# A recurrent attention block and an expert layer on one core: heads 0 to 3 and 4 to 7 in the two partition halves, read weights turned by way of DRAM, and new queue orders

## The chip, the cores and the metric

The kernel runs on one core of a Trainium2 chip. The metric is the device time of one launch in microseconds. Three runs of the kernel before took 720.58, 729.39 and 728.37 us, a median of 728.37.

A core has five engines that run side by side, each with a queue of its own: TensorE (PE, matmuls, with weight loads shown as PEld), VectorE (DVE), ScalarE (ACT), GpSimd (POOL) and SyncE (SP). SyncE computes nothing here; its queue issues most of the transfers, GpSimd's some, ScalarE's two at the start. All transfers run on the same 16 DMA engines.

## What is computed

```python
def _attn_ref(x, state):            # x (8, 8, 512, 64), state (8, 8, 32, 64)
    scale = 1.0 / np.sqrt(D)
    scores = scale * np.matmul(x, state.transpose(0, 1, 3, 2))
    a = softmax(scores)
    xread = np.matmul(a, state)
    scores2 = scale * np.matmul(state, x.transpose(0, 1, 3, 2))
    a2 = softmax(scores2)
    sread = np.matmul(a2, x)
    return np.concatenate([xread, sread], axis=2)

x = attn_out.transpose(0, 2, 1, 3).reshape(B * S, H * D)    # 4352 x 512
h = x @ w_in                        # 512 x 2048
g = h * erf(softplus(h))
out = g @ w_out                     # 2048 x 512
```

`softmax` stands for the usual steps (subtract the maximum of the row, exponentiate, divide by the sum plus 1e-9). The two weight matrices arrive as 64-bit floats.

## The kernel before

Eight batches are worked one after the other. A batch has 8 heads of 512 tokens and 32 states. Two heads fill the 128 partitions of the head dimension (2 x 64): before, heads 2i and 2i+1 are the pair i, head 2i in partitions 0 to 63 and head 2i+1 in partitions 64 to 127. Four heads of 32 states fill 128 partitions on the side of the states.

**Attention of a batch** (`attend`, L667 to L759). The tokens come in a form that VectorE can turn with its 32 by 32 transpose: `load_xq` (L88 to L93) makes 16 transfers for a batch, one for each head and each half of the head dimension, each of 64 KB in pieces of 32 elements. Each then is turned in place (L676), TensorE forms the scores (`score`, L684) and ScalarE copies them to `sc` (for odd batches) or to a part of `m` (for even ones). One softmax runs over the states of a token and one over the tokens of a state; the weights of the second (L724) are turned in 32 by 32 blocks (L746), and the blocks must then be exchanged between partition groups. `send` (L749 to L756) does it with 16 transfers of 32 KB from `xT` to `sc` or `m`. `read` (L773 to L792, matmul in L782) multiplies the turned weights with the tokens in a second layout, `x`, loaded by `load_x_static` (L765 to L768), 8 transfers a batch, one for each head.

**Expert layer.** `mixed` (L811, matmul in L820) multiplies the states with `w_in` first, so that the product with the softmax weights (`first_product`, L919) gives h directly. `serf` (L956, L959) forms h times erf of softplus of h. The second product runs in `second_product` (L1003) or, for the later batches, in `twice_product` (L1239). Both products use Strassen-like sums of blocks (`sums_y` L857, `sums_a` L970, and others), so VectorE has many adds.

**Weights.** A 64-bit weight is turned to 32 bits by two ScalarE and three VectorE instructions (`convert`, L542 to L550). The first half is fetched at the start on SyncE's queue (`fetch_pair`; `fetch_in` L525, `fetch_out` L533, and L559), the second half later on GpSimd's, in stages of one piece.

**The order of the work.** Nothing is issued where it stands in the code. `op` (L139) records each step with its engine, a cost, what it reads and what it writes. At the end `emit` (L291) walks five hand-given orders, one for each engine (`ORDER`, L163), in which the numbers are places in that engine's list of steps, and gives each step a time of beginning from the costs: a transfer may have a landing time (`land`) or a shared one (`pipe`: the transfers that have it pass one after the other). The instructions are then recorded in the order of these times, and `in_order` (L78) ties each engine to its order. So the costs decide no more than how the five orders interleave in the program; each engine's own order is that of `ORDER`. `either` (L156) gives some copies to VectorE (`BY_VECTOR`), the rest to ScalarE. Spare products (`spare_products`) keep TensorE busy at the start, before there is real work.

SyncE's queue is in order: a transfer that waits for its data, or for its destination to come free, holds all that are behind it. In the stretch that matters here, before, it holds the 16 transfers of `load_xq` for batch 2, 8 of `load_x_static` for batch 1, the 16 of `send` for batch 1, `kept_a` and `kept_y` (L864 and L865, which keep a batch's products for the second half of the kernel), the 16 of `load_xq` for batch 3, and so on in turn.

Of the kernel before, what the change touches and what calls it, by code (L numbers as in the profile page):

```python
# [17 lines left out]
def kernel(  # L18
# [17 lines left out]
    nc = tc.nc  # L36
# [51 lines left out]
    def load_xq(b, hs=range(H)):  # L88
        t = xq_t[b]
        for h in hs:  # L90
            i, e = h // 2, h % 2
            for k in range(2):
                nc.sync.dma_start(  # L93
                    out=t[D * e + Ns * k:D * e + Ns * k + Ns, i],
                    in_=x[b, h, :, Ns * k:Ns * k + Ns].rearrange("(m t) d -> t m d", t=Ns))
# [13 lines left out]
    where = {h: (g, q) for g, hs in enumerate(((0, 2, 1, 3), (5, 7, 4, 6)))  # L109
             for q, h in enumerate(hs)}  # L110
# [28 lines left out]
    def op(engine, cost, at, go, reads=(), writes=(), table=None, land=0.0, pipe=0.0):  # L139
# [14 lines left out]
        x2 st s01 m010 m011 m020 m021 u0 u1 m120""".split())  # L154

    def either(name, cost, out, in_, at, reads, writes):  # L156
# [3 lines left out]
        else:  # L160
# [4 lines left out]
            8 0 5 1-3 6 15 9 4 7 10 12 16 13 17 11 14 18 20-21 19 23 25 24 22 61 60 53 52 44-45 37  # L165
            26 46 28 27 29 36 47 62 31-32 30 54 68 48-49 51 50 34 33 41 35 38 69 40 70 55 39 43 72
            63 42 73 65 74 84 71 75 77 76 66 79-80 78 67 81 85 64 59 57 56 86 93 82-83 97 87 98 89
            88 58 94-96 90 99 101-102 121 100 122 124 103 123 125 109 105-106 128 126-127 107 131 91
            108 132 130 110 129 133 92 113-114 134 104 115 111 116 135 112 136 117-120 138 140-141
            168 142-143 171 144 169 145 170 146 148 172 147 149-150 137 175 173 151 156 178 139 174  # L170
            179 152-154 180 176 155 157 181 177 160-163 182 158-159 183 185 187 164-167 188-189 215
            190 216 191 218 195 217 184 219 199-200 220 201-202 192 221-222 193 196 225 194 186 197
            203 226 223-224 227 198 228-229 204-205 230 207-208 206 209 232 263 210 262 234-235 265
            236 231 266 211-212 264 237 233 267-269 213 270 272 271 214 273 242 246-248 238-239 275
            249 243 274 277 244-245 276 240-241 250-256 281 257 282-283 279 258 284 259 309 278 260
            289 312 261 311 313 290 310 285 314 316 291 315 293-294 318 295 286 280 319 296 287 320
            317 288 292 322 321 297 301 323 302-303 324 355 298-300 356 304 357 327 305-308 362 358
            329 328 334 359 325 335-336 330 360 337 326 331 338 361 365 339 364 332 366 340 363 367
            348 368 350 397-398 333 349 399 341 351 342-343 352 344-345 354 346 353 376 401 377-378
            400 379 347 380 402 369 381-382 371 370 373 403 372 404 374 390 405 375 406 383 392 409  # L180
            407 385 408 391 384 410 393-394 387 427 425 386 388 395 426 389 428 396 431-432 429
            433-434 413 430 415 435-436 423 437 416 421 438-439 414 440 455 419 424 457 422 458 456
            411 420 412 417 459 418 462 461 460 445 443 465 463 441 466 444 464 467-468 449 469 442
            470 453 447 454 450 448 499 446 451 502 501 452 478 500 503 471 506 480 473 504 472 479
            482 481 505 509 508 475 474 510 483 507 484 476 511 477 512-513 485 492 487 514 489
            493-494 543 495 486 488 546 490 545 496 491 544 498 547 497 522 515 550 549 517 548
            523-524 516 519 553 552 518 526 554 520 525 555 551 527-528 521 556 536 529 538 557-558
            531 530 537 540 539 533 587 532 534 542 589 541 566 588 568 567 590 570 535 571 591 559
            594 561 592-593 560 569 562 596-597 563 572 598 595 564 599-600 580 565 601 581-582 573
            602 583 631 575 574 584 576-577 634 633 578 585 579 586 603 635 610 632 605 636 611 604  # L190
            606 613 638 612 607 637 614 641 639-640 642 616 615 609 643 608 617 624 644-645 626 646
            625 619 675 618 628 627 621 620 629 676 678 630 677 679 622 654 623 655-656 680 682 658
            657 647 681 648 685 683-684 686 659 650 649 687 651 660 688-689 652-653 668 690 670 669
            661 720 719 672 671 721 662-664 673-674 665 722 666 726 723 698 667 700 699 701 724 702
            725 691 729 693 728 730 704 727 695 703 692 732 696 694 731 734 712 697 733 714 713 763
            715 705 716 765-766 707 706 718 717 764 767 708 770 709 768 710 742 711 743-744 769 735
            746 772 745 737 773 771 739 736 774 740 738 747 775 748 776 756 741 758 749 757 759 751
            750 752-753 760 754-755 762 777 761 784 778-779 786 781 780 785 782-783 788 791 787 793
            792 794-795 790 789 797-798 796 805 799-801 807 802 806 808-809 803-804 810-811""",
        ACT: """  # L200
            0-3 5 14-15 4 12-13 7 6 8 16 10 17 32-33 18-19 55 9 11 56 20-21 35 34 36 38 22-23 37 39
            24-25 41 40 26-27 43 42 44-45 28-29 47 49-50 46 48 64 53 61 58 57 51-52 54 59 66-67 65
            68-69 31 60 70 73 71 95 94 105 104 72 77 74 102-103 76 106 75 107 79 86-87 78 98 63 96
            80 100 97 99 83 82 101 81 84-85 90 135 88 91 134 136-137 145 110 139 62 138 109 89 92
            149 30 93 108 151 112 142 113 150 152 111 153 158 154-155 160 143 140 147 161 141 159
            163 115 156 162 114 164 144 166 146 157 148 165 172 171 116 167-168 173-174 176 175 186
            117-118 169 119 170 182 188 187 120 189 121 180 190 195 177 179 197 178 198 122 183 123
            191 194 181 192 201 184 124 199 125 202 196 200 203 193 204 185 208-209 205 210 212 211
            126 128 206 213 207 127 223 219 217 225-226 224 131 129 216 227 215 214 130 229 232 132
            234-235 133 233 238 236 230 220 239 218 221 237 240 228 231 246-247 245 248 241 249 242  # L210
            250 260 222 243 262 244 263 255 261 264 269 256 271 254 252 272 253 251 266 277 258 265
            268 270 273 267 274 276 284 282 285 275 278-280 257 281 259 283 287 286 293 297 299 290
            298 300 288 291 301 306 289 302 308 304 292 309 312 307 295 311 310 303 314 313 305 319
            315 321 320 322 294 316-317 344 296 318 324 345-346 329 347 325 348 330-331 323 353 327
            332 350 326 349 355 354 351 333 356 352 357 359 339 358 360 340 361-363 328 364 334 365
            335 342 341 386 337-338 336 343 371 373 372 374 366 375 367 369 388 368 381 370 389 382
            376 387 390 393 392 391 377 394-395 384 396 379 397 378 380 385 383 399 401 398 402-403
            400 406 405 413 412 415 414 417 404 407-411 418 422 419-421 426 424 428 425 429 423 427
            432 431 430 433-436 441 440 437 439 442 416 463 438 465 448 464 443 466 449 467 472 450
            444 451 473-474 446 475 445 471 469 476 479 447 486 453 480 452 468 454 458 477 470 478  # L220
            488 485 487 481 509 482 456 459 511 455 483 461 460 510 484 512 462 494 457 489 513 518
            490 515 495 492 520 491 514 521 516 497 493 496 517 524 519 498 522-523 525 504-505 526
            499 527 533-534 528 531 500 507 529 532 506 502 555 530 508 540 501 541 556-557 543 503
            558 535-536 559 564-565 544 542 566 538 563 567 561 537 560 570 569 568 550 562 571-573
            577 539 574 545 580 579 578 551 575 546 552 576 553 601 548 547 602 549 554 603 581 604
            586 582 607 588 605 610 608 584 587 589 583 612-613 585 611 615 591 614 590 606 596-597
            623 616 618 625-626 609 617 592 619 598 624 599 620 647 621 593 649 622 594 600 648 650
            632-633 651 634 595 627 635 656 658 657 659 653 628 654 660 636 629 652 630 662 669 631
            670 642 663 661 672 671 664 655 643 665 693 645 637 666 644 667 694 638 646 668 640 639
            695 641 696 678 680 679 697 681 702 673 704 674 699 705 708 682 676-677 703 701 675 706  # L230
# [1464 lines left out]
```

## Time and profile before

| | |
|---|---|
| runs | 720.58, 729.39, 728.37 us; median 728.37 |
| profiled execution | 719.11 us, its span 717.3 us, mean granted TensorE clock 0.99 |
| TensorE busy | 698.8 us, 97% of the span |
| VectorE busy | 593.4 us, 83% |
| ScalarE busy | 471.9 us, 66% |
| GpSimd busy | 85.7 us, 12% |
| transfers | 159615 packets, 89.22 MB, of them 124096 packets under 512 bytes |
| chain that ended last, by engine | PE 82%, DVE 4%, SyncE's queue 4%, DMA 1%, ACT 1% |
| `load_xq`, SyncE | 112 transfers of 64 KB, 3.1 us from issue to landing (median) |
| `load_x_static`, SyncE | 56 of 128 KB, 3.6 us |
| `send`, SyncE | 64 of 32 KB to `sc`, 1.9 us, and 48 to `m`, 2.0 us |
| `kept_a`, SyncE | 8 of 512 KB, 3.9 us |

The busy times of engines overlap. A busy TensorE row counts matmuls that are in the pipeline, so two instructions that overlap are not counted twice. Idle time of an engine that is not the limit costs nothing. The granted clock is the share of full speed at which TensorE was let run.

### The profile page before, as it was taken

To read this page: it belongs to the slowest core of one execution; us is meant where nothing else is said; L and a number is where in the kernel's file an instruction comes from. 1 tells how busy PE (TensorE), PEld (TensorE's weight loads), DVE (VectorE), ACT (ScalarE), POOL (GpSimd) and SP (SyncE) were. 2 spreads that over 40 slices of the span, in tenths; PEclk is the share of its full clock that TensorE was granted. 3 is DMA by queue.
4 is the path that set the end of the run, shared out by engine and by line. 5 is a ranking of instruction groups with operands and counts; after the bars stand their busy time and mean duration, and the time that the engine had idled before them with its cause. 6 is when DMAs were issued, how large, how long until landed. Compare 5 with 4: busy or idle time off the path is not lost.

```text
span 717.3 us, 13372 instructions
## 1 busy us (share of the span) xinstructions
PE 698.8 (97%) x5163; PEld 581.6 (81%) x5163; DVE 593.4 (83%) x989; ACT 471.9 (66%) x850; POOL 85.7 (12%) x93
## 2 busy tenths in 40 slices
PE   8899979999999999999999999999999999999997
PEld 7434647788787868789999779898989898989996
DVE  4999969999999899697975479686969587789797
ACT  4996976978767575657444765667585577676732
POOL 0001100111001000000100100013222104312321
PEclk9899998999999999999999999999999999999999
DMA  8858596989576934240486402124545503735485
GB/s 271 204 142 189 125 229 162 235 206 237 92 192 219 255 82 132 48 131 1 119 198 225 92 0 81 52 30 91 80 81 60 101 11 85 104 42 67 58 141 104
DMA packets 159615, 89.22 MB, mean 124 GB/s; under 512 B 124096, under 2 KB 147520, under 8 KB 159040
## 3 DMA queue, kind: packets, MB, share of 16 engines
q1 hardware_dynamic: 140208, 58.22, 31.5%
q0 software_dynamic: 18800, 29.63, 22.2%
q8 instruction: 41, 0.67, 0.4%
q10 hardware_dynamic: 544, 0.52, 0.2%
q14 instruction: 22, 0.18, 0.1%
HBM read 47.19 MB, written 37.49 MB: 118 GB/s over the span
## 4 chain that ended last, share of the span: by engine, by line
PE 82%; DVE 4%; SPq 4%; DMA 1%; ACT 1%; issue 1%; DVEq 0%; ACTq 0%
PE o L1239 30%; PE h L919 17%; PE o L1003 15%; PE at L919 7%; PE o L1422 3%; PE h L1373 3%; SPq L93 2%; PE h L820 2%; PE at L820 2%; SPq L754 1%; PE h L684 1%; PE at L1373 1%; PE at L782 1%; DVE ring L970 1%; PE o L622 1%
## 5 line engine op out<-in xcount | busy, mean ns | idle before, releaser
L931 ACT COPY ring<-h 128x512 f32<-128x512 f32 x120 | 69.5, 584 | 80.2 <-PE h L919 69.4
L919 PE MATMUL h<-aT,m 128*128 128x256 f32 x360 | 92.1, 382 | 0.1
L959 DVE TENSOR_TENSOR ring<-ring 128x1024 f32<-128x1024 f32 (+1 forms) x64 | 72.9, 1150 | 18.1 <-ACT ring L956 18.0
L941 ACT ACTIVATE ring<-ring 128x512 f32<-128x512 f32 x120 | 72.3, 631 | 10.9 <-PE o L1003 2.6
L1003 PE MATMUL o<-w_out,ring 128*128 128x256 f32 x320 | 77.6, 383 | 1.3 <-DVE ring L959 1.3
L919 PEld LDWEIGHTS h<-aT,m 128*128 128x128 f32 x360 | 65.4, 190 | 12.7 <-issue 1.8
L1003 PEld LDWEIGHTS o<-w_out,ring 128*128 128x128 f32 x320 | 60.1, 191 | 16.5 <-issue 3.0
L970 DVE TENSOR_TENSOR ring<-ring 128x1024 f32<-128x1024 f32 x60 | 72.9, 1216 | 0.3
L1239 PE MATMUL o<-w_out,w_in 128*128 128x128 f32 x512 | 69.2, 276 | 0.0
L1239 PEld LDWEIGHTS o<-w_out,w_in 128*128 128x128 f32 x512 | 64.5, 192 | 1.9 <-issue 0.3
L1239 PE MATMUL o<-w_out,ring 128*128 128x128 f32 x480 | 65.1, 276 | 0.0
L1239 PEld LDWEIGHTS o<-w_out,ring 128*128 128x128 f32 x480 | 60.5, 192 | 4.3 <-issue 0.8
L956 ACT ACTIVATE ring<-ring 128x1024 f32<-128x1024 f32 (+1 forms) x64 | 63.3, 1008 | 0.2
L1003 PE MATMUL o<-raw,ring 128*128 128x256 f32 x240 | 59.2, 386 | 0.0
L1003 PEld LDWEIGHTS o<-raw,ring 128*128 128x128 f32 x240 | 45.5, 192 | 11.2 <-issue 3.4
L1239 PE MATMUL o<-raw,ring 128*128 128x128 f32 x360 | 48.5, 275 | 0.0
L1239 PEld LDWEIGHTS o<-raw,ring 128*128 128x128 f32 x360 | 45.3, 192 | 1.7 <-DVE oo L1254 0.8
L1159 POOL DMA_DIRECT2D out_dram<-oo x16 | 24.4, 1585 | 151.1 <-ACT ring L956 115.0
L1239 PE MATMUL o<-raw,xT 128*128 128x128 f32 x320 | 41.7, 276 | 0.0
L1239 PEld LDWEIGHTS o<-raw,xT 128*128 128x128 f32 x320 | 38.8, 192 | 2.1 <-ACT o L1270 1.7
L622 PE MATMUL o<-w_out,ring 128*128 128x512 f32 x64 | 31.0, 607 | 0.1
L919 PE MATMUL at<-sy,sx 128*128 128x256 f32 x120 | 31.0, 381 | 0.0
(267 smaller groups left out, 1401.1 us busy)
## 6 DMA issues: line engine op xcount, KB each, us to landing
xq<-in_x_dram SPq DMA_DIRECT2D x112, 64.0 KB, 3.1
x<-in_x_dram SPq DMA_DIRECT2D x56, 128.0 KB, 3.6
out_dram<-oo SPq DMA_DIRECT2D x10, 512.0 KB, 3.7
raw<-in_moe_w_in_dram SPq DMA_DIRECT2D x8, 512.0 KB, 6.9
raw<-in_moe_w_out_dram SPq DMA_DIRECT2D x4, 1024.0 KB, 6.5
raw<-in_moe_w_out_dram POOLq DMA_DIRECT2D x8, 512.0 KB, 6.0
raw<-in_moe_w_in_dram POOLq DMA_DIRECT2D x8, 512.0 KB, 6.7
kept_a<-aT SPq DMA_DIRECT2D x8, 512.0 KB, 3.9
```

What stands on the lines that cost most here:

```text
L622: nc.tensor.matmul(out=bank("o%d" % r), lhsT=gT[g][:, i, P * r:P * r + P], rhs=w_out[:, GF * g + i, :], start=(made_of[r] == 1), stop=(mad ...
L820: nc.tensor.matmul(out=bank(names[k])[Ns * p:Ns * p + Ns, :], lhsT=st[r, b, q], rhs=of_group[2 * u + j][r, :, i, :], start=True, stop=True)
L919: nc.tensor.matmul(out=out_[:, i], lhsT=x_[:, q:q + P], rhs=y_, start=(start and i == 0), stop=(i == 1), skip_group_check=not start)
L931: op(ACT, 0.5, t, lambda: nc.scalar.copy(out_(), view(bank(name))), [name], w)
L941: op(ACT, 0.53, t, lambda: nc.scalar.activation(out=part(splane, k), in_=part(hplane, k), func=ACTF.Softplus), area(hplane, ks=[k], os=[o] ...
L956: op(ACT, 0.085 + 0.875 * share, at + n, lambda s_=s_: nc.scalar.activation(out=s_, in_=s_, func=ACTF.Erf), [], area(splane, ks=[k], os=os ...
L959: op(DVE, 0.065 + 1.075 * share, at + n + 1, lambda s_=s_, h_=h_: tt(s_, s_, h_, op=ALU.mult), area(hplane, ks=[k], os=os), area(splane, k ...
L970: op(DVE, 1.14, at + k, lambda k=k, x_=x_, y_=y_, how=how: tt(get("h", k), get(*x_), get(*y_), op=how), area(v[x_[0]], ks=[x_[1]]) + area( ...
L1003: nc.tensor.matmul(out=view(name)[:, h], lhsT=lhs[:, i, :], rhs=weight_of[n]()[:, u, i, :], start=(start and h == 0 and i == 0), stop=(h = ...
L1159: op(GP, 1.2, t, lambda: nc.gpsimd.dma_start(out=quad(r, c), in_=one(v), accum_op=ALU.add), every(*v), [("out", b, r, c)], land=6.0)
L1239: nc.tensor.matmul(out=out_[:, Q2 * k:Q2 * k + Q2], lhsT=lhs[:, k, i], rhs=rhs[:, i], start=first, stop=(k == len(ns) - 1 and i == 1), ski ...
L1373: nc.tensor.matmul(out=bank(bk)[:, P * i:P * i + P], lhsT=x_[:, i, k], rhs=y_[:, k], start=(start and i == 0 and k == 0), stop=(i == GF - ...
```

## The change

It has four parts.

1. **Heads.** Heads 0 to 3 now lie in partitions 0 to 63 and heads 4 to 7 in partitions 64 to 127, so that pair i is heads i and 4+i. One transfer can then load four heads: `load_xq` makes 4 transfers for a batch instead of 16, the states of batches 1 to 7 come in 2 instead of 8, and the rows of `w_in`, which have to follow the heads, in two halves of 64 partitions for each piece instead of one transfer of 128 partitions. The tokens in the layout of `read` come two heads at a time, 4 transfers instead of 8.
2. **Read weights.** The exponentials of the second softmax are written in another order, so that after the 32 by 32 turn one transfer puts the whole `xT` half (128 x 1024) into a DRAM tile, `kept_t`, and four transfers bring it back, each to 32 partitions. These replace the 16 transfers from `xT` to `sc` or `m`.
3. **Costs of transfers in the plan.** Nearly all transfers get a share of a common DMA time (`pipe`) instead of a landing time of their own, and SyncE's queue is held to 4 us ahead of it (`AHEAD`).
4. **Orders.** All five orders in `ORDER` and the list `BY_VECTOR` are new. The same matmuls, and but for the transfers nearly the same instructions, stand in other places.

The core of the diff (the five orders, which make up most of it, and changed costs left out):

```diff
-    def load_xq(b, hs=range(H)):
+    def load_xq(b, first=0, n=NI):
         t = xq_t[b]
-        for h in hs:
-            i, e = h // 2, h % 2
+        for e in range(2):
             for k in range(2):
+                q, h = D * e + Ns * k, NI * e + first
                 nc.sync.dma_start(
-                    out=t[D * e + Ns * k:D * e + Ns * k + Ns, i],
-                    in_=x[b, h, :, Ns * k:Ns * k + Ns].rearrange("(m t) d -> t m d", t=Ns))
+                    out=t[q:q + Ns, first:first + n].rearrange("t i m d -> t (i m) d"),
+                    in_=x[b, h:h + n, :, Ns * k:Ns * k + Ns].rearrange(
+                        "i (m t) d -> t (i m) d", t=Ns))
...
     BY_VECTOR = set("""
-        x2 st s01 m010 m011 m020 m021 u0 u1 m120""".split())
+        x0 x1 x2 s10 ta1 m021 u1""".split())
...
-    FIXED = 2.6
+    FIXED, AHEAD = 2.2, 4.0
...
                     if pipe:
-                        piped = max(piped, end[n]) + pipe
-                        end[n] = piped + FIXED
+                        piped = max(piped, begin[n]) + pipe
+                        end[n] = max(piped, free[e]) + (land or FIXED)
+                        if e == SP:
+                            free[e] = max(free[e], piped - AHEAD)
...
+    def rows_in(on, to, f, n):
+        for e in range(2):
+            on.dma_start(out=to[D * e:D * e + D],
+                         in_=moe_w_in[NI * D * e:NI * D * (e + 1), P * f:P * (f + n)].rearrange(
+                             "(k d) f -> d k f", d=D).bitcast(U32))
...
-            for h in range(4 * k, 4 * k + 4):
-                i, e = h // 2, h % 2
-                nc.sync.dma_start(out=st[Ns * i:Ns * i + Ns, 1:B, D * e:D * e + D],
-                                  in_=state[1:B, h].rearrange("b n d -> n b d"))
+            nc.sync.dma_start(out=st[:, 1:B, D * k:D * k + D],
+                              in_=state[1:B, NI * k:NI * k + NI].rearrange(
+                                  "b i n d -> (i n) b d"))
...
             op(ACT, 0.7, at + 6, lambda e=e: nc.scalar.activation(
-                out=both()[:, 2 + e], in_=sc()[:, e], func=ACTF.Exp,
+                out=both()[:, 2:4].rearrange("p k t -> p (k t)").rearrange(
+                    "p (m e c n) -> p e c m n", m=NI, e=2, c=NC)[:, e],
+                in_=sc()[:, e].rearrange("p (c m n) -> p c m n", c=NC, m=NI), func=ACTF.Exp,
                 bias=m2()[:, e:e + 1], scale=scale, accum_out=z2()[:, e:e + 1]),
...
         def send():
-            blocks = both()[:, 0:2].rearrange("p e (c m n) -> p m (e c) n", m=NI, n=Ns)
-            rows = sc().rearrange("p e (c i n) -> p i (e c) n", c=NC, n=Ns)
+            nc.sync.dma_start(out=kept_t[b % 2], in_=both()[:, 0:2].rearrange("p k t -> p (k t)"))
+
+        def receive():
+            blocks = kept_t[b % 2].rearrange("(i t) (m x) -> m t i x", t=Ns, m=NI)
             for m in range(NI):
-                for i in range(NI):
-                    nc.sync.dma_start(out=rows[Ns * m:Ns * m + Ns, i],
-                                      in_=blocks[Ns * i:Ns * i + Ns, m])
-
-        op(SP, 11.0, at + 10, send, ["xT0", "xT1"], [sc_of(b, 0), sc_of(b, 1)], land=4.0)
+                nc.sync.dma_start(out=square()[Ns * m:Ns * m + Ns], in_=blocks[m])
+
+        op(SP, 0.5, at + 10, send, ["xT0", "xT1"], ["kt%d" % (b % 2)], pipe=1.4)
+        op(SP, 2.1, at + 14, receive, ["kt%d" % (b % 2)], [sc_of(b, 0), sc_of(b, 1)], pipe=1.7)
...
-        for h in range(H):
-            nc.sync.dma_start(out=t[:, :, h, :], in_=x[b, h].rearrange("(c p) d -> p c d", p=P))
+        for h in range(0, H, 2):
+            nc.sync.dma_start(out=t[:, h:h + 2].rearrange("p h c d -> p (h c) d"),
+                              in_=x[b, h:h + 2].rearrange("h (c p) d -> p (h c) d", p=P))
```

In the changed kernel the lines named above stand a little lower: the score matmul is L689, the turning of x L681, the read matmul L794, the first 512-column matmul of the start L602 (L597 before), the store to `kept_t` L758 and the transfers back L763; L93 is still the load of x.

More of the change, by code (lines that the diff above doesn't have):

```diff
@@ L108 @@
     raws = [act.tile([P, 2 * 2 * d_model], U32, name="raw", bufs=3) for _ in range(3)]
-    where = {h: (g, q) for g, hs in enumerate(((0, 2, 1, 3), (5, 7, 4, 6)))
-             for q, h in enumerate(hs)}
+    head = lambda e, i: NI * e + i
     def warm(out, n, by=ident):
@@ L170 @@
[L170 to L174, printed above, removed]
@@ L306, in emit @@
                     begin[n] = max([free[e]] + [end[m] + LAG[ops[m][0]] * (
-                        ops[m][0] != e or ops[m][6] + ops[m][7] > 0) for m in needs])
+                        ops[m][0] != e or ops[m][7] > 0) for m in needs])
                     if table not in (None, loaded):
@@ L576, in go @@
         def go():
-            for h in range(H):
-                i, e = h // 2, h % 2
-                k, p = where[h]
-                nc.tensor.matmul(out=bank(banks[k])[Ns * p:Ns * p + Ns, 0:n * P],
-                                 lhsT=st00[D * e:D * e + D, Ns * h:Ns * h + Ns],
-                                 rhs=of_group[g][D * e:D * e + D, first:first + n, i, :],
-                                 start=True, stop=True)
+            for i in range(NI):
+                for e in range(2):
+                    q = P * e + Ns * i
+                    nc.tensor.matmul(out=bank(banks[e])[Ns * i:Ns * i + Ns, 0:n * P],
+                                     lhsT=st00[D * e:D * e + D, q:q + Ns],
+                                     rhs=of_group[g][D * e:D * e + D, first:first + n, i, :],
+                                     start=True, stop=True)
         fs = range(first, first + n)
@@ L865, in keep_y @@
                                  nc.sync.dma_start(out=kept_y[b], in_=static["sy%d" % (b % 2)])),
-           aT_of(b) + sy_of(b), ["kept%d" % b], land=3.0)
+           aT_of(b) + sy_of(b), ["kept%d" % b], pipe=2.4)
     def bring_y(b, at):
@@ L873, in go @@
             nc.sync.dma_start(out=static["sy%d" % (b % 2)], in_=kept_y[b])
-        op(SP, 1.1, at, go, ["kept%d" % b], aT_of(b) + sy_of(b), land=5.0)
+        op(SP, 1.1, at, go, ["kept%d" % b], aT_of(b) + sy_of(b), pipe=2.4)
     def seven(product, regions, cost, names, s_of, at, apart, step):
@@ L1175, in store @@
                 op(SP, 0.4, t, lambda: nc.sync.dma_start(out=quad(r, c), in_=mine(r, c)),
-                   own(r, c), [("out", b, r, c)], land=2.2)
+                   own(r, c), [("out", b, r, c)], pipe=0.8)
             for r in range(2):
@@ L1289, in twice_product @@
                     out=quad(0, 1)[:, h, cols], in_=mine(0, 1)[:, h, cols]),
[L1290 removed]
+                   area(final, us=[0], ks=[2 + h], os=range(qs.start, qs.stop)), [], pipe=0.2)
             return
```

316 lines of the change are left out of this document (157 added, 159 removed), and 3 rows, old and new, of the table ORDER.

## The prediction

> **What bounds the kernel now.** I read the page's busy line first, then busy time by stretch, then the longest waits, then SyncE's own timeline and the chain.
>
> ```profile
> PE 698.8 (97%) x5163; PEld 581.6 (81%) x5163; DVE 593.4 (83%) x989; ACT 471.9 (66%) x850; POOL 85.7 (12%) x93
> ```
>
> TensorE is busy 97% of the span, so only its idle and slowed stretches can be saved. By stretch (columns: start:end, width, then busy us of PE, PEld, DVE, ACT, POOL, the granted clock, the DMA engines' share, GB/s):
>
> ```profile
> 18.00:24.00 6.00, 3.43 (x25) 2.28 (x26) 5.79 (x15) 5.26 (x11) 0.00 (x0) 0.64 0.74 192
> ...
> 90.00:96.00 6.00, 6.00 (x33) 4.28 (x39) 5.89 (x14) 5.66 (x12) 0.55 (x1) 1.00 1.07 333
> 96.00:102.00 6.00, 4.67 (x44) 2.45 (x29) 3.83 (x6) 5.90 (x10) 0.00 (x0) 1.00 0.84 178
> 102.00:108.00 6.00, 2.37 (x16) 1.11 (x18) 2.40 (x5) 1.15 (x2) 0.00 (x0) 0.75 0.86 172
> 108.00:114.00 6.00, 6.00 (x30) 3.89 (x17) 5.74 (x12) 3.17 (x6) 0.55 (x1) 0.68 0.65 142
> ```
>
> TensorE idles in two places: the first 24 us, and 96 to 108, where it loses 1.33 + 3.63 = 5.0 us. After each the granted clock falls, to 0.64 and to 0.68. VectorE is over 95% busy around the second hole, so it is the next limit. Who ended the hole:
>
> ```profile
> PE h L684 <- DVE xq L676: 3.6, 1, 3.6
> DVE xq L676 <- DMA xq<-in_x_dram: 5.7, 2, 4.9
> ```
>
> The scores of batch 3 (L684) wait for VectorE's turning of x (L676), and that for the load of x (L93). Why the load is late stands in SyncE's queue:
>
> ```profile
> 73.13 11.46 SPq L754 DMA_DIRECT2D sc<-xT  x16
> 84.64 0.60 SPq L864 DMA_DIRECT2D kept_a<-aT  x1
> 85.28 0.43 SPq L865 DMA_DIRECT2D kept_y<-sy  x1
> 85.81 17.52 SPq L93 DMA_DIRECT2D xq<-in_x_dram  x16
> ```
>
> Sixteen issues move the read weights in 11.5 us, and the sixteen of the x load behind them take 17.5 us: the queue is bound by the number of issues. By the same view TensorE idles 2.0 us in all from 30 to 96 us, and after 112 us only 1.25 us near 256 and the last 5 us; what is recovered early reaches the end.
>
> **The change, part by part.** The sum is made against the profiled execution: 719.1 us, span 717.3.
>
> *Work.* The same 2611 matmuls and, within three, the same VectorE and ScalarE instructions. SyncE's transfers fall from 371 to 188; GpSimd gets eight more (each late w_in piece is two halves). GpSimd is 12% busy; eight more at 1 us cost nothing while it waits for others, 8 us of its own time if that cover went.
>
> *The hole at 96 to 108.* The read weights become 1 issue, two kept transfers, and 4 issues; the x load 4 instead of 16. By L864 one issue is 0.6 us, by L93 0.5. After the turned weights at 73.1: send to 73.7; its 512 KB land like `kept_a` (3.9 us) at 77.0; four issues to 79.1; x issued to 81.2. Moving the x is not cheaper: 8192 packets of 128 bytes at 12.8 ns over 16 engines are 6.6 us. Landing about 2.5 us later gives 90, against 105.4. The scores need it in TensorE's queue not before 95 (below). So the hole goes. Its price: 5.0 idle, plus half speed from 105.0 to 111.8, by the two clocks 6 x 0.25 + 6 x 0.32 = 3.4 us, of which 0.7 lie in the idle: 2.7; plus 1.0 because L684 took 3.07 us there against 1.02 elsewhere. Together **-8.7**.
>
> *The start.* Three copies of x (0.6 each) pass to VectorE, which idles until 6.7, and ScalarE reaches the first w_in words earlier. These land at about 8.0 (issued 1.74, 6.3 us). Following the queues: ScalarE converts 8.1 to 9.3, VectorE's three conversions end at 10.7 (now 13.2), first softmax half 10.7 to 11.9, second w_in 13.9, second half's weights ready at 19.7 (now 22.1). What VectorE did before that point is equal to 0.2 us, so its work moves forward whole: **-2.4**. Bounds: 0 if the w_in halves land later (the DMA engines run at 1.06 of their share from 6 to 12 us), -4.1 if the half-speed stretch after 18 us (6 x 0.36 and 6 x 0.21 are 3.4, about half of it outside the idle: 1.7) goes too.
>
> The Trainium skill, "DMA: Bandwidth & Descriptors", "Rules for kernel authors", speaks against the halves: two transfers to disjoint partition halves serialize, and one of 128 partitions is better. By it the split buys nothing and adds an issue to each piece; the sum would be some 0.5 us worse here. No row before shows a 64-partition transfer.
>
> *The read weights' way through DRAM.* A new wait: SyncE stands at the receiving transfers until the store has landed, and the next x loads queue behind it. The trip is 0.2 + 3.9 (store) + 1.5 (three issues) + 1.9 to 3.6 (by the small `sc<-xT`, or a 128 KB `x` load): 7.5 to 9.2, I take 8.5, since `kept_a` and `kept_y` pass beside it. Is it hidden? I add up what stands ahead of an instruction in its queue, at durations of before (256 columns 0.43, 512 0.86, a VectorE 512 0.6). An instruction then runs at that sum plus a constant: before, 12.2 for TensorE and 11.8 for VectorE at 66 to 97 us; after, 2.4 less, so 9.8 and 9.4.
> Batch 2: TensorE has 22 fewer L1003 and 10 fewer L919 matmuls ahead of the read, 91.3 instead of 105.1; VectorE is done with the weights at 80.9, mostly since nine instructions of weight conversion move behind. Ready at 90.3, needed at 101.1: 10.8 us of cover. Batch 1: 71.7 and 84.5, 12.8. Batch 6: 245.4 and 254.8, 9.4, the thinnest. I take 0, with +5 as the upper bound.
>
> *The rest of the new orders.* The 1.25 us hole at 256 (a store of `oo` and VectorE) I leave; bounds -1.3 and 0. New waits somewhere in 550 us of a full TensorE: none is visible in the sums, I take **+1.0** (bounds 0 and 4; batch 3 in before cost 3.6).
>
> Sum: -8.7 - 2.4 + 1.0 = -10.1, so **709.0 us** for an execution like the profiled one. The runs shown are 1.5, 9.3 and 10.3 above theirs, the median 728.4. What differs between them no profile shows; a hole that hangs on landing times and ends in a half-speed stretch is the kind of thing that differs, and it goes. I carry half of the median's distance, 4.6: **713.6 us**. Two per cent, about what a measurement of this kernel can tell from no change, is 14.6 us, so 713.8 to 742.9 is "the same".
>
> The Trainium skill's "TensorE: Matmul & The Clock Gate", "Part 1", has the clock halved after an idle window of 3.4 us that runs free of the kernel. The fall after a 3.6 us hole agrees. By it, executions of one kernel may differ by one such stretch, and start waits of 1.3 to 1.6 us, as I find them after, need not halve the clock: 1.7 us less than my sum.
>
> **The rivals.** First number like the profiled execution, second like the median.
> - *The trip through DRAM is too long* (the other side). The send stands behind the x load of the batch before in the same queue, 4096 packets of 256 bytes at 19.5 ns, 5.0 us of the engines; added to 9.2 this is 14. From there the reads of batches 1, 2, 6 and 7 (covers 12.8, 10.8, 9.4, 10.7) wait 1.2 + 3.2 + 4.6 + 3.3 = 12.3, and one half-speed stretch adds 2.7: 719.1 - 10.1 + 15 = 724.0. As the transfer wait is then still there, the whole 9.3 is carried: 733.3, slower than before. For it: before showed one load of x taking 17.5 us for 6.6 us of packets. Against: at 90 us, by my walk, that x load has just been drained. Below a trip of 9.4 it costs nothing; it decides from 13.
> - *VectorE is the bound.* It gains only its own idle, 2.17 + 3.60, and the start: -5.8 - 2.4 + 1.0 gives 711.9, 716.5. For it: 95% in both neighbours. Against: its converted weights move back behind batch 2.
> - *The start gains nothing* (w_in halves late): 711.4, 716.0.
> - *The spread was the hole's own.* The runs then lie 1.5 above 709.0: 710.5.
> - *The change doesn't do what it says*: the x load stays late because its 8192 packets, not the issues, set it. Half of the hole remains: -4.4 - 2.4 + 1.0, 713.3, and with the spread 722.6.
>
> **How the numbers follow.** Forecast 0.30, DRAM trip 0.12, VectorE 0.15, start 0.15, no spread 0.20, late load 0.08. Predicted 713.6. Low end 704: both start bounds and 256 us won (-8.7 - 4.1 - 1.3 = 705.0, less a little of the run spread). High end 730: above the late load, and the milder half of the DRAM case. Faster by over 2%: all of "no spread", two thirds of the forecast, a little of the next two: 0.45. Slower by over 2%: needs the DRAM case with a second slowed stretch, or several new holes: 0.07. Within 2%: 0.48.
>
> **What would show it.** Right: no DVE wait on `xq` at L681 above 1 us near 90 to 105 us, L93 taking about 2 us for four issues, one granted-clock fall at most, TensorE's group of reads for batch 2 ending near 102 instead of 127.5, VectorE's second softmax weights at 19.7. Wrong: a TensorE wait at the read (L794) for `sc` or `m` from `kept_t`, SyncE standing over 6 us at L763, a start that reaches the first 512-column matmul (L602) later than 21.5, or TensorE idle above 3 us after 112 us.

## The result and the profile after

The changed kernel takes 709.0 us (median of four executions, 708.3 to 710.5); the kernel before takes 724.5 (median of four, 717.3 to 729.4, among them the three named ahead of the prediction). The ratio is 0.986, with a 95% interval of 0.982 to 0.991; it leaves out the two slow executions of before (728.4 and 729.4 us), so it is nearer to 1 than the medians are. The profiled execution took 708.3 us with a span of 706.5, against 719.1 and 717.3 before: 10.8 us less. So the predicted 713.6 lay 4.6 us too high, and the sum made for a profiled execution, 709.0, was 0.7 too high. That the sum came so close is partly luck, as the terms below show.

The busy line of the page of the changed kernel:

```profile
PE 693.0 (98%) x5163; PEld 579.7 (82%) x5163; DVE 592.3 (84%) x986; ACT 469.6 (66%) x852; POOL 89.8 (13%) x101
```

The 5163 records of matmuls are as many as before; the 5.8 us of busy time that are gone are the half-speed stretch and slowed matmuls. Busy time by stretch, with the columns as before (PE, PEld, DVE, ACT, POOL, granted clock, DMA share, GB/s):

```profile
18.00:24.00 6.00, 2.48 (x28) 1.63 (x28) 4.77 (x10) 3.50 (x6) 0.00 (x0) 0.93 1.07 268
...
90.00:96.00 6.00, 5.98 (x50) 3.17 (x48) 5.97 (x11) 5.97 (x13) 0.00 (x0) 1.00 1.00 185
96.00:102.00 6.00, 6.00 (x45) 4.10 (x38) 5.86 (x11) 5.97 (x12) 0.00 (x0) 1.00 1.06 328
102.00:108.00 6.00, 6.00 (x87) 5.02 (x87) 5.96 (x13) 5.69 (x10) 0.00 (x0) 1.00 1.07 168
108.00:114.00 6.00, 6.00 (x30) 5.24 (x29) 5.97 (x13) 5.14 (x10) 0.00 (x0) 1.00 1.12 206
```

The hole at 96 to 108 us is closed: TensorE is full, at clock 1.00, where it lost 5.0 us and then ran at 0.75 and 0.68. The start has not gained: TensorE has 2.48 us of work from 18 to 24 us, against 3.43 before, and 24 to 30 still runs at 0.78. SyncE's queue, which explained the hole:

```profile
76.30 0.35 SPq L758 DMA_DIRECT2D kept_t<-xT  x1
...
82.10 1.75 SPq L763 DMA_DIRECT2D sc<-kept_t  x4
83.95 5.35 SPq L93 DMA_DIRECT2D xq<-in_x_dram  x4
89.40 4.73 SPq L779 DMA_DIRECT2D x<-in_x_dram  x4
95.15 0.34 SPq L758 DMA_DIRECT2D kept_t<-xT  x1
...
99.06 1.76 SPq L763 DMA_DIRECT2D m<-kept_t  x4
100.92 6.85 SPq L93 DMA_DIRECT2D xq<-in_x_dram  x4
```

Send and receive take SyncE 7.6 us from 76.30 to 83.85 (the two stores of `kept_a` and `kept_y` lie inside, and 4.1 us of standing until the store to `kept_t` has landed), where 16 issues took 11.5. The x load is the surprise: its four issues take 5.35 and 6.85 us, not about 2. Their number does not explain that: in the load at 83.95 the first issue took 0.38 us and the next three 2.02, 1.25 and 1.52. It points to the packets that are under way, since the whole is near the 6.6 us that its 8192 packets need; four issues that start at 57.5 us, with the DMA engines idle, also take 5.3 us. The x of batch 3 is turned from 93.8 us on all the same, and its scores run at 98.1 without a wait.

To see where TensorE lost or won time I add up, in the order of its queue, the full-speed durations of all matmuls ahead, and subtract that from the time at which an instruction ends (its lag, in us):

```
at about                        95      115     240     270     end of matmuls
before                         12.4    21.1    23.1    25.3    39.5
after (first value: at 84 us)  12.4    13.2    14.5    15.2    29.4
```

Before 84 to 95 us the two are equal; in the hole 7.9 us are won, from 115 to 240 us 0.7, at the small hole near 256 us 1.5, after it nothing, and the tail behind the last matmul is 0.7 shorter (5.3, now 4.5). Together 10.8, as the spans say.

### The profile page after: what moved, and what is told of

Same layout as the page of the kernel before. It is cut to its first block, busy times and chain, and to the rows that moved or that the text cites. A ratio compares the mean times of both kernels' runs of the same rounds, so it can differ in the third digit from the quotient of the medians.

```text
span 706.5 us, 13126 instructions
## 1 busy us (share of the span) xinstructions
PE 693.0 (98%) x5163; PEld 579.7 (82%) x5163; DVE 592.3 (84%) x986; ACT 469.6 (66%) x852; POOL 89.8 (13%) x101
## 4 chain that ended last, share of the span: by engine, by line
PE 84%; DVE 6%; DMA 2%; ACT 2%; issue 1%; DVEq 0%; SPq 0%
PE o L1250 28%; PE h L930 18%; PE o L1014 17%; PE at L930 7%; PE o L1433 4%; PE h L1384 3%; DMA raw<-in_moe_w_out_dram 2%; PE h L831 2%; PE at L831 2%; PE at L794 1%; PE at L1384 1%; PE h L689 1%; DVE w_in L1232 1%; DVE ring L981 1%; DVE ring L970 1%
## 5 line engine op out<-in xcount | busy, mean ns | idle before, releaser
L1281 ACT COPY o<-o 128x256 f32<-128x256 f32 (+1 forms) x41 | 13.5, 330 | 26.8 <-PE o L1250 17.8
L930 PE MATMUL h<-sy,m 128*128 128x256 f32 x120 | 31.1, 382 | 0.0
```

Of the source, the lines that this page charges most:

```text
L930: nc.tensor.matmul(out=out_[:, i], lhsT=x_[:, q:q + P], rhs=y_, start=(start and i == 0), stop=(i == 1), skip_group_check=not start)
```

## The experiments

The runs below were made on four chips, each time beside the kernel before, which takes 720.1 to 721.8 us there (medians); the changed kernel, run again on one of them, takes 709.1. Absolute times of the changed form are compared with that 709.1. Packet durations are means over the trace's DMA records, for packets that start in the stretch named.

**The changed kernel again.** No edit.

> The changed kernel itself, on one chip with the next two. Expected: 707.5 to 710.5, its runs within 3 us of each other. If the spread of before's runs came from the hole at 96 to 108 us, before's runs here spread by 8 us or more and these do not; if it came from the chip, both spread alike.

Measured: 709.1 us (706.6 to 710.0, six executions), ratio to before 0.981 (0.977 to 0.985); before spread from 718.3 to 727.7 beside it, 9.4 us against 3.3. So the narrow spread is a property of the changed kernel and not of a chip. What is left of it can be seen in the two profiled executions, 708.3 and here 706.9 us. In the second one the half-speed stretch fell earlier (12 to 18 us, clock 0.72), onto TensorE's idle time, and the eight L602 records that follow took 3.70 us instead of 5.21. A window that runs free of the kernel, as the Trainium skill's "TensorE: Matmul & The Clock Gate", "Part 1", has it, would do this. The records:

```profile
23.22 3.70 PE L602 MATMUL h<-aT,m 128*128 128x512 f32 x8 [0.81 <-ACT m L161]
```

**Transfers without the new orders.** The changed transfers and tiles, with the orders of before:

```
-    ORDER = { ... orders of the changed kernel ... }
+    ORDER = { ... orders of before; SP: each receive behind its send and that batch's stores ... }
```

> The changed kernel's transfers and layouts with the orders of before on every engine (each receive right behind its send and the stores of that batch). Theory, the transfers alone remove the hole: TensorE's idle from 96 to 108 us below 1 us, one half-speed stretch only, the 256 us hole of about 1.5 us back, 709 to 712. Rival, the orders were needed as well: VectorE or the wait of SyncE at the receive keeps half of the hole, 713 to 718.

Measured: 718.1 us (717.1 to 719.3), ratio 0.996 (0.993 to 0.998). The theory fell; the rival's 713 to 718 was nearer. TensorE's waits (us in total, times, longest) and the stretch of the old hole:

```profile
PE at L582 <- DVE ring L615: 3.6, 1, 3.6
PE o L1011 <- DVE ring L967: 2.7, 2, 2.2
PE at L791 <- DMA m<-kept_t: 2.6, 1, 2.6
```
```profile
102.00:108.00 6.00, 3.80 (x22) 2.38 (x29) 4.26 (x8) 4.03 (x8) 0.00 (x0) 1.00 1.10 284
```

The hole shrinks to 2.2 us and keeps the clock at 1.00, but L1011 now waits for VectorE there, the start has a wait of 3.6 us near 40 us (VectorE's product in L615), and a read (L791) waits 2.6 us near 271 for the way through DRAM. With the old orders that trip is too long for its cover. The wait of 3.6 us goes back further: VectorE stands behind ScalarE, and ScalarE behind a late piece of `w_in`:

```profile
37.20 1.14 ACT L544 ACTIVATE w_in<-raw 128x1024 f32<-128x1024 f32 x1 [2.88 <-DMA raw<-in_moe_w_in_dram]
```

So part of what this run loses may be the price of the halves of `w_in`, which it has too (below), and not of the old orders. No run here has the old orders without the halves.

**New orders without the transfers.** All in the new orders: the read weights by 16 direct transfers (as many as before, but in pieces of 1024 bytes and not of 128), the x load of batches 2 to 7 by 16, and both. The halves of `w_in` and the other new transfers stay. The edits:

```
         def send():
-            nc.sync.dma_start(out=kept_t[b % 2], in_=both()[:, 0:2].rearrange("p k t -> p (k t)"))
+            blocks = both()[:, 0:2].rearrange("p k t -> p (k t)")
+            for m in range(NI):
+                for i in range(NI):
+                    nc.sync.dma_start(out=square()[Ns * m:Ns * m + Ns, i],
+                                      in_=blocks[Ns * i:Ns * i + Ns, 2 * P * m:2 * P * m + 2 * P])
         def receive():
+            pass
 ...
     def load_xq(b, first=0, n=NI):   # for n == NI: one transfer per head instead of one per four
```

> The changed kernel, its orders kept, with the read weights sent by 16 transfers from tile to tile without DRAM (L758, L763) and the x load of batches 2 to 7 by 16 transfers instead of 4. Theory, the number of issues on SyncE made the hole: the 32 issues take 25 us or more again, TensorE idles 3 to 6 us somewhere from 95 to 115 us and gets a second half-speed stretch, 6 to 10 us more than the changed kernel: 715 to 719. Rival, the new orders of the engines removed it: no idle above 1 us there, 708 to 711.

> The changed kernel with the read weights alone in 16 direct transfers (L758, L763); the x load keeps its 4. Theory, issues on SyncE add up: 11 us of issues end later than the trip through DRAM (last issue 5.3 us behind the send), batch 2's read waits 4 to 5 us, and so do one or two later batches: 8 to 15 us over the changed kernel, 717 to 724. Rival, a threshold: each half of the change alone has enough slack and only both together cost the 34 us; then within 4 us of 709.

> The changed kernel with the x load of batches 2 to 7 alone in 16 transfers; the read weights keep the way through DRAM. Theory, issues on SyncE add up: 11 us instead of 5.4 to 6.9 for each load, x and the sends behind it 4 to 6 us later; batch 3's scores and batch 2's read wait: 8 to 20 us over the changed kernel, 717 to 729. Rival, the loads are bound by their 8192 packets and not by issues: within 3 us of 709.

Measured: both 742.8 us (739.8 to 743.5), the read weights alone 727.8 (725.1 to 731.2), the x load alone 713.4 (711.2 to 717.7); ratios to before 1.029 (1.026 to 1.033), 1.007 (1.004 to 1.010) and 0.986 (0.981 to 0.992). SyncE's queue with both:

```profile
79.13 11.32 SPq L762 DMA_DIRECT2D sc<-xT  x16
...
91.65 10.67 SPq L95 DMA_DIRECT2D xq<-in_x_dram  x16
102.42 2.86 SPq L782 DMA_DIRECT2D x<-in_x_dram  x4
105.39 10.70 SPq L762 DMA_DIRECT2D m<-xT  x16
```

The sign of all three theories holds and none of their sizes: both cost 34 us and not 6 to 10, the read weights alone 18.7 and not 8 to 15, the x load alone 4.3 and not 8 to 20, which is close to its rival (within 3). The trains of issues are about as long as foreseen (11 us each), but with the new orders the queues have less room for them: with both, TensorE idles 35.7 us in all against 13.5, and 16.7 of these lie after 112 us. The read weights' issues are the costly ones, and together the two cost 10.7 more than their sum. Part of it is the clock: with the read weights alone, five stretches below full speed lose 10.3 us (6 us times what the clock lacks, summed), against 1.7 in the changed kernel.

The four corners, old and new orders by old and new transfers, are 720.7 and 718.1, 742.8 and 709.1 (the corner of 742.8 has only the two trains of 16 issues back, not the other old transfers). The new transfers without the new orders are worth 2.6 us, the new orders with these old transfers cost 22, both changes together win 11.6. Neither is the cause by itself: the orders are written for these transfers.

**A longer trip.** The read weights go through a second DRAM buffer:

```
+            nc.sync.dma_start(out=kept_u[b % 2], in_=kept_t[b % 2])
...
-            blocks = kept_t[b % 2].rearrange(...)
+            blocks = kept_u[b % 2].rearrange(...)
```

> The changed kernel with the read weights' trip lengthened by a second copy inside DRAM (512 KB, 4 to 6 us more). Theory, the trip of batch 2 (sent at 95.15, read at 104.5) uses its cover to the last 0.3 us: batch 2 waits 4 to 6 us, batches 1, 6 and 7 1 to 5 us each, and SyncE's later loads too: 8 to 15 us over the changed kernel, 717 to 724. Rival, the covers of the prediction (1 to 4 us left above a trip of 8.5): 1 to 5 us over, 710 to 714.

Measured: 730.1 us (726.6 to 734.9), 21 more than the changed kernel and above the theory's 8 to 15; ratio to before 1.010 (1.007 to 1.014). TensorE's waits:

```profile
PE at L796 <- DMA sc<-kept_u: 9.3, 3, 5.0
PE at L796 <- DMA m<-kept_u: 3.4, 1, 3.4
```

Four reads wait 12.7 us together, and stretches below full speed lose 12.0 us instead of 1.7. Batch 2's weights, for one, leave at 103.14 and are read at 116.09 after a wait of 3.4: a trip of 13.0 us with a cover of 9.5. In the changed kernel they leave at 95.15 and are read at 104.5, with a wait of

```profile
PEld at L794 <- DMA m<-kept_t: 0.3, 1, 0.3
```

There the trip is 9.3 us long and the cover about 9.1. It just fits. The second copy is also 512 KB more for the DMA engines and holds SyncE until the first store has landed (2.7 us at batch 2), so the 21 us are not the price of the longer trip alone.

**The start: one transfer per piece, and two halves in the old row order.**

```
     def rows_in(on, to, f, n):
+        if on is nc.sync:                                   # one transfer per piece
+            on.dma_start(out=to, in_=moe_w_in[:, P * f:P * f + P].rearrange(
+                "(k p) f -> p k f", p=P).bitcast(U32))
+            return
```
```
+        if on is nc.sync:                                   # two halves, old row order
+            rows = moe_w_in[:, P * f:P * f + P].rearrange("(k p) f -> p k f", p=P)
+            for e in range(2):
+                on.dma_start(out=to[D * e:D * e + D], in_=rows[D * e:D * e + D].bitcast(U32))
+            return
```

> The changed kernel with each of the eight early w_in pieces as one transfer of 128 partitions, in the row order of before (so rows of w_in meet other heads than in the reference: the amount of work and data is the same). Theory, the halves made the start late: the 1024-byte packets cost about 50 ns again instead of 75 to 81, ScalarE's 2.9 us wait at 20.5 us (L549 for raw) falls below 1 us, VectorE's second softmax weights come near 20, TensorE's first matmul of L602 near 22 instead of 23.5, and the time is 1.5 to 2.5 us below that of the changed kernel, 706.5 to 707.5. Rival, the new order of SyncE's queue (1 MB of w_out ahead of the third and fourth w_in piece) made it late: the wait stays above 2 us and the time within 0.7 us of 709.

> The changed kernel with each early w_in piece in two 64-partition transfers as there, but with the row order of before (rows k*128+p, so rows of w_in meet other heads than in the reference, as in the run with one transfer per piece). It separates the two things that changed in a piece. Theory, writing to 64 partitions is what is slow: 1024-byte packets at 75 to 81 ns, third and fourth piece near 20 us, 708 to 710. Rival, the new order of the rows in DRAM is what is slow: packets near 50 ns, TensorE's first matmul of L602 by 22, 704 to 706.

Measured: one transfer per piece 704.7 us (702.5 to 705.4), ratio to before 0.976 (0.973 to 0.980), 4.4 us under the changed kernel and more than the theory gave. Two halves in the old row order 709.1 (706.9 to 710.1), as the changed kernel. (In these two, rows of `w_in` meet other heads: they price the transfer and are no versions to keep.) The 1024-byte packets from 5 to 12 us, nearly all of them w_in, take

```
before 49.6 ns, changed 76.7 (run again: 73.3), one transfer per piece 50.5, halves in the old row order 78.2
```

The DMA engines are full in that stretch in all of them and move less with the halves (last two columns: share and GB/s; changed kernel, one transfer per piece, halves in the old row order):

```profile
5.00:12.00 7.00, 6.50 (x103) 5.00 (x102) 4.20 (x7) 3.18 (x7) 0.00 (x0) 1.00 1.11 254
```
```profile
5.00:12.00 7.00, 6.28 (x103) 4.78 (x102) 4.41 (x7) 4.07 (x9) 0.00 (x0) 1.00 1.07 372
```
```profile
5.00:12.00 7.00, 5.77 (x101) 4.20 (x100) 4.67 (x8) 2.85 (x7) 0.00 (x0) 1.00 1.10 242
```

It is the form in two 64-partition transfers that is slow, not where the rows lie in DRAM. Whether the 64 partitions do it or that there are two transfers, these runs do not separate. A piece of 512 packets over 16 engines takes 2.3 to 2.5 us of the engines instead of 1.6. What that does to ScalarE, in the changed kernel (its timeline; the bracket is the idle time before and what ended it):

```profile
20.50 1.17 ACT L549 ACTIVATE raw<-raw 128x1024 uint32<-128x1024 uint32 x1 [2.86 <-DMA raw<-in_moe_w_in_dram]
...
22.73 0.58 ACT L161 COPY aT<-o 128x512 f32<-128x512 f32 x1
23.19 0.28 ACT L161 COPY m<-h 128x128 f32<-128x128 f32 x1
```

and TensorE's first matmuls of that line, in the kernel before (L597), in the changed kernel (L602) and with one transfer per piece (L606):

```profile
23.17 4.42 PE L597 MATMUL h<-aT,m 128*128 128x512 f32 x6
```
```profile
23.52 5.21 PE L602 MATMUL h<-aT,m 128*128 128x512 f32 x8 [1.76 <-ACT m L161]
```
```profile
21.40 1.02 PE L606 MATMUL h<-aT,m 128*128 128x512 f32 x2
22.78 2.84 PE L606 MATMUL h<-aT,m 128*128 128x512 f32 x6 [0.36 <-DVE aT L159]
```

They begin 2.1 us earlier and, at full speed, end 3.1 us earlier (25.62 against 28.73). The clock is part of it: its mean lacks 0 to 2.1 us of the span in the four executions with one transfer per piece, and 2.1 to 5.0 in the ten of the changed kernel. One part of the start is not the halves' doing. ScalarE now converts the first words at 7.4 us instead of 8.4, and the second softmax weights still come at 20.9 (21.0 in the changed kernel), since VectorE's first conversion stands behind its third copy of x:

```profile
8.80 0.69 DVE L159 COPY xT<-o 128x512 f32<-128x512 f32 x1 [0.57 <-PE o L404]
9.40 0.42 DVE L555 TENSOR_SCALAR w_in<-w_in 128x512 uint32<-128x512 uint32 x1
```

The price with which the new orders were planned fits this too: the operation that fetches a piece (`fetch_in`) carries `pipe=1.7` us in the changed kernel, right for 1.6 and 0.6 to 0.8 short here, for each of eight pieces.

**The start: other ways to fill 128 partitions.** The second half of the first two pieces issued by ScalarE, and each piece as four transfers `[2, 64, 256]` over all partitions:

```
-            on.dma_start(out=to[D * e:D * e + D],
+            (nc.scalar if on is nc.sync and e and f < 2 else on).dma_start(out=to[D * e:D * e + D],
```
```
+            for k in range(NK):
+                on.dma_start(out=to[:, k], in_=moe_w_in.rearrange(
+                    "(e k d) f -> k e d f", e=2, k=NI)[k, :, :, P * f:P * (f + n)].bitcast(U32))
```

> The changed kernel with the second half (partitions 64 to 127) of the first two w_in pieces issued by ScalarE, so that both halves move at the same time. Theory, a 64-partition transfer is slow by itself and two at once are not: packets near 50 ns from 5 to 9 us, the first piece lands about 1 us earlier (ScalarE's conversion at 7.6 instead of 8.4 us), the start gains 1 to 2 us: 707 to 708. Rival, the packets stay at 75 to 81 ns since the bytes per partition half set them: no change, 708 to 709.5, or a loss of up to 1 us from two more issues on ScalarE.

> The changed kernel with each early w_in piece in four transfers of all 128 partitions, one per 64-row block of each half (32 issues instead of 16; the same layout, rows and heads as in the changed kernel). Theory, the 64-partition form is what is slow: 1024-byte packets near 50 ns, clock 1.00 after 18 us, and within 1.5 us of the run with one transfer per piece: 704 to 706. Rival, the number of issues on SyncE is what counts in the start: four issues per piece take 2 to 3 us each, the third and fourth piece land later than 20 us and the time is 709 to 712.

Measured: two queues 708.4 us (706.9 to 709.1), ratio 0.982 (0.979 to 0.985), no gain that can be told from 709.1; packets at 5 to 12 us 72.0 ns, against 76.7 and 73.3. So the theory of two queues fell. The Trainium skill, "SBUF — State Buffer", "Can I just issue two DMAs to hit both halves?", has the same: two concurrent transfers, at partitions 0 and 64, gained only 6% over one, and only one transfer over all 128 partitions reaches all ports. The 2 to 6% that a second queue gains here in packet time agree; that ports are the reason no run here shows.

The four transfers cost far more than either theory foresaw: 782.8 us (782.6 to 784.4), ratio 1.082 (1.077 to 1.087). SyncE, eight issues (the third and fourth piece):

```profile
23.77 23.20 SPq L527 DMA_DIRECT2D raw<-in_moe_w_in_dram  x8
```

2.9 us for each. Its packets take 48 ns, and 128 of them over two engines are 3.1 us, over 16 engines 0.4. The transfer ran on about two engines: from 5 to 12 us the share of the 16 is 0.13, or 2.1 engines.

```profile
5.00:12.00 7.00, 4.17 (x63) 3.27 (x62) 2.07 (x3) 0.37 (x1) 0.00 (x0) 1.00 0.13 46
```

So the run does not answer what it was made for, the price of the 64 partitions. The Trainium skill, "DMA: Bandwidth & Descriptors", "Rules for kernel authors" (use all 16 engines), says that an outermost dimension below 16 confines a transfer to at most as many engines; here it is 2, and the trace agrees.

**The start: other orders.** Two conversions of the late pieces moved behind the copies that TensorE waits for:

```
         ACT:  ... 16-17 30 9 31
-              15 33 14 8 32 19 ...
+              33 8 32 15 14 19 ...
         DVE:  ... 11-13 24 76
-              21 14 22-23 ...
+              14 21 22-23 ...
```

> The changed kernel with two conversions of the third and fourth w_in piece (L549, L547) moved behind three copies (m, m, aT; L161) in ScalarE's order, and one copy (aT, L159) moved ahead of L551 in VectorE's; nothing else. Theory, the late w_in pieces cost time because ScalarE stands 2.9 us at L549 and the copies that TensorE's first L602 matmul needs are queued behind: that matmul starts near 20.5 instead of 23.5, TensorE gains 1.5 to 2.5 us, and 1.7 more if the half-speed stretch goes: 705 to 707.5. Rival, VectorE's second softmax weights (21.0) set the start: within 0.7 us of the changed kernel.

> The run above with the second half of the first two w_in pieces issued by ScalarE as in the run with two queues. Theory, the two gains add (0.6 there): 704.5 to 707. Rival, ScalarE's two issues now delay its first copies: no better than the run above.

Measured: 707.8 us (706.6 to 708.3) and 707.7 (706.6 to 709.5); ratios 0.980 (0.976 to 0.984) for both. That is 1.3 under the changed kernel by medians, with overlapping ranges. TensorE does begin earlier:

```profile
22.12 5.30 PE L602 MATMUL h<-aT,m 128*128 128x512 f32 x8
```

by 1.4 us, but not at 20.5, since turning the second softmax weights waits for VectorE first. The order of ScalarE's queue was one part of the loss in the start; the transfers' own length remains, and two queues add nothing. These two are the fastest versions here that keep the kernel's layout, by little. No run here has a piece in one transfer of 128 partitions with the new rows; it would need a transfer of four dimensions.

## Why the prediction was right and wrong

- **The hole, -8.7.** Right: 7.9 by the lags. TensorE does not wait for x, and one fall of the clock is gone. The reason given, the number of issues, holds for the read weights. For the x load it holds in part: sixteen issues take 9.5 to 10.3 us, but four still take 5.35 and not 2, so "x issued to 81.2, landing 90" became 89.3 and about 93. It was hidden, as the scores came at 98.1. The reads of batch 2 ended at 105.6 and not near 102.
- **The start, -2.4: the step that failed.** By the lags it came to 0. The walk put the first w_in words at 8.0 us (measured 8.4) and the second softmax weights at 19.7 (measured 21.0), and said that a start beyond 21.5 would prove it wrong; it was 23.5. The larger cause is the term taken as free, the halves' own transfer time: 73 to 78 ns a packet for 50. With one transfer per piece the matmuls begin at 21.4 and, by the same lags, the start wins about 2.5 us. The rival "w_in halves late" was right, and the runs price the halves at 4.4 us, where the prediction had 0.5 for the extra issues. The rule that the prediction cites against the halves, in the Trainium skill's "DMA: Bandwidth & Descriptors", "Rules for kernel authors", is to use one transfer of 128 partitions; that agrees. The walk's 19.7 is a second error, since it is missed by 1.2 us without the halves too: among other things, the walk left out that VectorE waits for its third copy of x before it converts (its three conversions end at 11.4 and not 10.7). The start waits that "need not halve the clock" went with a fall of it in the profiled execution: two of 1.76 us, with 0.66 us of matmuls between them, and half speed from 23.2 to 26.6 us.
- **The trip through DRAM, 0.** Right in its result: TensorE waits 0.3 us for it and SyncE stands 4.1 us at most. Its length was 9.3 us where 8.5 was taken, and batch 2's cover 9.1 where the sum gave 10.8, so the margin of 2.3 us was none. The rival on the other side was close: it decides "from 13" us, and with the second copy the trip was 13.0 at batch 2 and the time 21 us longer.
- **New waits, +1.0, and the 256 us hole, left.** Both wrong by a little and in the same direction: no new waits (TensorE idles 0.45 us from 112 to 700 us, and 115 to 240 us won 0.7), 1.5 won near 256, 0.7 in the tail. What closed these was not separated. They made up for the start.
- **The spread, +4.6: the other failed step.** The forecast took the median of three executions, 728.4, for what before takes, and carried half of its distance from the profiled 719.1. In the 49 executions of before beside the experiments the median is 721.3, so the distance was 2 us and not 9. Nor did any of it stay: the changed kernel's ten executions lie within 3.9 us of each other, before's within 8.7 to 9.4 on each of four chips. "The spread was the hole's own" would have said 710.5. The granted clock goes with it: before's three slowest of the 49 (727.7 to 728.7 us) had a mean clock of 0.981 to 0.983, its three fastest (718.3 to 718.5) 0.989 to 0.992, which is some 6 of the 10 us between them. What started the extra half-speed stretches is not in any trace here, so the cause stays open. Idle time as such does not make it: with the old orders and new transfers TensorE idles 19.7 us in all (18.5 in before), and nine executions lie within 2.2.

## What to carry to other kernels

An order written for one set of transfers is part of those transfers: change one without the other and the gain is lost or turned round, so price both together, with transfer times from a trace of the new form. Count a transfer by the partitions it reaches and by its outermost dimension before counting its issues: two transfers of half the partitions cost 1.5 times the packet time of one over all, an outermost dimension of 2 left about two engines working. A wait that just fits its cover (9.3 us in 9.1) is free only until something makes it longer.

## What the runs showed of the hardware

- From 5 to 12 us a 1024-byte packet took 72 to 83 ns in the eleven traces where the pieces came in two transfers of 64 partitions, and 50 in the two where they came in one of 128, whatever the order of the rows in DRAM. Two halves at once, from two queues, took 72. The full DMA engines moved 219 to 271 GB/s in the one form and 351 to 372 in the other.
- A transfer `[2, 64, 256]` words went at about two engines' rate, 2.9 us for 128 KB.
- The x load's four issues (8192 packets of 128 bytes) held SyncE for 5.3 to 6.9 us from 57 us on, sixteen issues of the same packets with the same orders for 8.5 to 10.7: with few issues the queue was still held up, for about as long as the packets need.
- The same kernel's half-speed stretch lay at 12 to 18 us in one execution and at 23 to 27 in another, 1.5 us apart in eight matmuls. By the clock records of the traces the clock was full or half, and half for 3.41 us or a whole multiple of it at a time (up to 23.9), but for the stretch that the end of the span cuts.
